# Attention rows turned to token order by 16-bit DMA transposes in place of TensorE transposes

## The chip, the cores and the metric

The kernel runs on one core of a Trainium2 chip. The metric is the device time of one execution in microseconds (us); lower is better. The core has a matrix engine (TensorE, PE in the profile; PEld is its weight load), a vector engine (VectorE, DVE), a scalar engine (ScalarE, ACT), a general engine (GpSimd, POOL) and a sync engine (SyncE, SP) that here only issues DMAs. Sixteen DMA engines serve all queues. The engines run their own instructions in program order and wait for each other by semaphores.

## What is computed

Attention with normalised queries and keys comes first, then a mixture of experts with a capacity. The batch is 8, with 12 heads, 448 positions and a head size of 64, so there are 3584 tokens of 768 values; 8 experts take at most 80 tokens each.

```python
q_n, k_n = (rmsnorm(q, g_q), rmsnorm(k, g_k))
scores = scale * np.matmul(q_n, k_n.transpose(0, 1, 3, 2))
attn = softmax(scores)
x = np.matmul(attn, v).transpose(0, 2, 1, 3).reshape(N, D)
...
logits = x @ w_gate
expert_idx = np.argmax(logits, axis=1)
gate_w = probs[np.arange(N), expert_idx]
for e in range(E):
    tok_idx = the tokens of expert e, the 80 of largest gate_w
    h = np.maximum(x[tok_idx] @ w1[e], 0.0)
    out[tok_idx] = gate_w[tok_idx, None] * (h @ w2[e])
```

All other rows of the output are zero.

## The kernel before

**Groups and half-steps.** The attention runs over 24 groups: a batch b and four of its heads, g = 3b + i. For each group, seven key blocks of 64 positions are gone through. The loop over `s` from -10 to NS + 5 (NS = 84) is a schedule written out by hand: in each half-step it scores two key blocks (`score`), adds up the exponentials of two earlier ones (`presum`) and multiplies two earlier ones with v (`av`). A group takes 3.5 half-steps. Everything else is hung into these half-steps with `at_slot`, in three places: `begins` (ahead of the scores; loads and other DMAs), `mid` and `end` (behind the products with v). b0 = 7g // 2 is a group's first half-step. Its q and k are loaded at b0 - 11, squared from b0 - 7, its v loaded at b0 - 4.

**The result of a group.** `av` gathers the unnormalised product in PSUM; at the group's last key block, in half-step b0 + 4, ACT copies it to the tile `us` of 128 partitions (two heads by 64 values) by 2 x 448 columns (positions), three buffers. Columns are positions and partitions are features there. The experts need rows: one token's 768 values together. `xout(g, u)` (L594 to L615) does that turn: PE transposes four blocks of 128 columns (L601) into the PSUM tile `xp`, of a pool of two buffers that it shares with the transposes of q and k (`tp`) and of the gate (`zt`); ACT copies `xp` to `xb` (L606), which has one buffer. It is called for u = 0 and u = 1 in two half-steps that follow each other. After the second, SP issues three DMAs (L614, L615) that store `xb` to the scratch `xr_scratch` in HBM; for the last group POOL issues them. A row of the scratch has 768 values and the 12 reciprocal sums of the token's softmaxes (`rz`, L418), as 32-bit floats.

**The gate.** From `us` and the sums, `zl` and the `gate` functions form logits, weights and, by ranking, the list of kept tokens of each expert. For batches 0 to 6 they lie among the half-steps of the next groups.

**The last batch and the experts.** Behind the loop stands a chain for the last batch, up to `idxG` (L835), the kept tokens. PE runs fillers meanwhile, `busy(n)`: n matmuls into the tile `hot` that nobody reads. Then POOL issues gathers by `idxG` from `xr_scratch` (L859), four ahead. `xpose(e)` multiplies the gathered rows by their reciprocal sums (`xn`, DVE, L868), transposes them on PE to `pxt` (L875) and copies them to `xgT` (DVE, L878). Each expert then runs a first product `ph` (L893) in two halves, each followed by ACT's `h_sb` (L897), then `xpose` of the next expert, then a second product `py` (L912); DVE scales it to `yo` (L917) and POOL scatters it to the output (L925).

**Weights and zeros.** The weights of experts 0 to 2 are loaded early. Those of experts 3 to 7 are cast to 16 bits in a scratch by POOL's DMAs during the attention (`stage_w`) and come in late from SP (`fetch_late`, L195); those of expert 5 in two parts, the first at L842 and L843, ahead of the gathers, behind a `memset` on DVE that holds it back. 28 DMAs of SP write zeros over the output.

Of the kernel before, what the change touches and what calls it, by code (L numbers as in the profile page):

```python
# [10 lines left out]
F32 = mybir.dt.float32  # L11
# [2 lines left out]
ALU = mybir.AluOpType  # L14
AX = mybir.AxisListType
U32 = mybir.dt.uint32
I32 = mybir.dt.int32
PSUM = bass.MemoryType.PSUM

# [2 lines left out]
def kernel(  # L22
# [36 lines left out]
    FC = F // 128  # L59


    XW = DM + H
    xr_dram = nc.dram_tensor("xr_scratch", (N, XW), F32, kind="Internal").ap()
    NW0 = 3
    wb_dram = nc.dram_tensor("wb_scratch", (E - NW0, 2, 128, DC * F), BF16,
                             kind="Internal").ap()
# [6 lines left out]
    ident = cpool.tile([128, 128], F32, name="ident")  # L73
# [97 lines left out]
    w_tiles = {}  # L171
# [30 lines left out]
    tpps = ctx.enter_context(tc.tile_pool(name="tp_ps", bufs=2, space=PSUM))  # L202
# [6 lines left out]
    prep = ctx.enter_context(tc.tile_pool(name="prep", bufs=2))  # L209
# [6 lines left out]
    with av_stack:  # L216
# [3 lines left out]
        st = [dict() for _ in range(NG)]  # L220
# [175 lines left out]
        def gate1v(b):  # L396
            zt = gst[b]["zt"]
            NT = NJ + 1
            ztv = zt[:, :].rearrange("p (j r) -> p j r", r=128)
            rz = gpool.tile([128, NT, H], F32, tag="rz", name="rz")  # L400
            for u in range(2):
                c = 64 * (1 - u)
                nc.vector.reciprocal(
                    rz[:].rearrange("p j (i u hh) -> p j u i hh", u=2, hh=2)[:, :, u],
                    ztv[:, :, c:c + 64].rearrange("p j (hh r) -> p j r hh", hh=2)[
                        :, :, 24:24 + NQ])
            lx = gpool.tile([128, NT, H, E], F32, tag="lx", name="lx", bufs=1)
            for u in range(2):
                for hh in range(2):
                    r = 64 * hh + 32 * u  # L410
                    nc.vector.tensor_mul(
                        lx[:].rearrange("p j (i k) e -> p j k i e", k=4)[:, :, 2 * u + hh],
                        ztv[:, :, r:r + NQ * E].rearrange("p j (i e) -> p j i e", e=E),
                        rz[:].rearrange("p j (i k) -> p j k i", k=4)[:, :, 2 * u + hh]
                        .unsqueeze(3).to_broadcast([128, NT, NQ, E]))
            gst[b]["lx"] = lx
            for t in range(2):
                (nc.sync if b < B - 1 else nc.gpsimd).dma_start(  # L418
                    out=xr_dram[b * S:(b + 1) * S, DM:XW].rearrange(
                        "(p x) h -> p x h", x=NX)[:, t::2],  # L420
                    in_=rz[64 * t:64 * t + 64, :NJ + 1 - t])

        def gate2(b):
            NT = NJ + 1
# [166 lines left out]
            return [[row, lambda: vbeat((0, 1))], [experts, lambda: vbeat((2, 3)), vtied],  # L591
                    [own, vahead], [counts, vput], [place], [turn]]

        def xout(g, u):  # L594

            b, i = divmod(g, NQ)
            xp = tpps.tile([128, 512], F32, tag="tp", name="xp")
            us = st[g]["us"]
            for j in range(NJ + 1):
                c = j * 128 if j < NJ else S - 128  # L600
                nc.tensor.transpose(xp[:, j * 128:(j + 1) * 128], us[:, u, c:c + 128],  # L601
                                    ident[:, :])
            if u == 0:
                st[g]["xb"] = prep.tile([128, NJ + 1, 256], F32, tag="xb", name="xb", bufs=1)
            xb = st[g]["xb"]
            nc.scalar.copy(xb[:, :, u * 128:(u + 1) * 128],  # L606
                           xp[:, :].rearrange("p (j d) -> p j d", d=128))
            if u == 0:
                return
            rows = xr_dram[b * S:(b + 1) * S, i * 256:(i + 1) * 256].rearrange(  # L610
                "(p x) d -> p x d", x=NX)
            eng = nc.sync if g < NG - 1 else nc.gpsimd
# [39 lines left out]
        for g in range(NG):  # L652
            b0 = g * RD // 2
            odd = g % 2
            at_slot(begins, max(b0 - 11, -10), load_qk, g)
            at_slot(begins, b0 - 4, load_v, g)
            if g:
                for a in range(2):
                    at_slot(mid, b0 - 7 + a if g > 1 else -1, square, g, a)
                    at_slot(end, b0 - 7 + a if g > 1 else -1, squares, g, a)  # L660
                at_slot(mid, b0 - 5 if g > 1 else 0, rstd, g)
                for a in range(2):
                    at_slot(mid, b0 - 5 + a if g > 1 else 0, normalise, g, a)
            for a in range(2):
                for f in range(2):
                    t = b0 - 4 + 2 * a + f
                    if g == 0 and a + f < 2 or g == 0 and a > f:
                        continue
                    if g < 2:
                        t += 2 if g == 1 and a + f == 0 else 1  # L670
                    at_slot(end, t, transp, g, a, f)
            at_slot(end, b0 + 4 + odd, xout, g, 0)
            at_slot(end, b0 + 5 + odd, xout, g, 1)
        for b in range(B):
            b0 = (NQ * b + NQ - 1) * RD // 2
            if b == B - 1:
# [67 lines left out]
    mpool = ctx.enter_context(tc.tile_pool(name="moe_sb", bufs=2))  # L744
# [12 lines left out]
    b = B - 1  # L757
# [26 lines left out]
    for j in range(NT):  # L784
        src = psb[:, 0, :] if j == 0 else row[:, :]
        c = min(j * 128 + 128, S)
# [41 lines left out]
    for k, (w, x) in enumerate(moves):  # L828
        for c0, c1, o in ((0, 3, 0), (3, 4, 1), (4, 5, 1)):
# [20 lines left out]
    xgs, xts = {}, {}  # L850
    def gather(e):

        if e % 4 == 3:
            xgs[e] = prep.tile([128, NJ + 1, 256], F32, tag="xb", name="xg", bufs=1)[
                :CAP].rearrange("p j d -> p (j d)")[:, :XW]
        else:
            xgs[e] = upool.tile([128, 2, S], F32, tag="us", name="xg")[:CAP].rearrange(
                "p u s -> p (u s)")[:, :XW]
        nc.gpsimd.indirect_dma_start(  # L859
            out=xgs[e], out_offset=None, in_=xr_dram[:, :],  # L860
            in_offset=bass.IndirectOffsetOnAxis(ap=idxG[:, e:e + 1], axis=0))

    def xpose(e):
        xg = xgs[e]
        xn = mpool.tile([CAP, DM], BF16, tag="xn", name="xn")
        for i in range(NQ):
            c = slice(256 * i, 256 * i + 256)
            nc.vector.tensor_mul(  # L868
                xn[:, c].rearrange("p (hh u d) -> p u hh d", hh=2, u=2),
                xg[:, c].rearrange("p (u hh d) -> p u hh d", hh=2, u=2),  # L870
                xg[:, DM + 4 * i:DM + 4 * i + 4].rearrange("p (u hh) -> p u hh", hh=2)
                .unsqueeze(3).to_broadcast([CAP, 2, 2, D]))
        pxt = mps.tile([128, DC, CAP], BF16, tag="pxt", name="pxt", bufs=1)
        for c in range(DC):
            nc.tensor.transpose(pxt[:, c, :], xn[:, c * 128:(c + 1) * 128],  # L875
                                identb[:CAP, :CAP])
        xgT = mpool.tile([128, DC, CAP], BF16, tag="xgT", name="xgT")
        nc.vector.tensor_copy(xgT[:], pxt[:])  # L878
        xts[e] = xgT

    for e in range(4):
        gather(e)
    xpose(0)
    busy(2)
    for e in range(E):
        w1_sb, w2_sb = w_tiles[e]
# [12 lines left out]
        if e + 1 < E:  # L899
            xpose(e + 1)  # L900
# [8 lines left out]
        for dn in range(2):  # L909
# [6 lines left out]
            c = DN if e + 1 < E or dn == 0 else DN // 2  # L916
# [5 lines left out]
        if NW0 + 3 + e < E:  # L922
# [42 lines left out]
```

## Time and profile before

Three executions took 476.2, 476.17 and 473.38 us; the median is 476.17.

| | us |
|---|---|
| median of three | 476.17 |
| profiled execution, time | 471.95 |
| its span in the profile | 469.9 |
| DVE copy xgT L878, mean of 8 (480 columns) | 0.41 |
| DVE reading py to yo L917, mean of 16 (384 columns) | 0.60 |
| ACT copy of 512 columns, L606 | 0.59 |
| ACT copy of 896 columns, us L346 | 0.90 |
| row stores of xb by SP, 192 KB and 64 KB, issue to landing | 7.0 and 5.3 |
| gathers xg, issue to landing, least and median | 3.4 and 8.2 |
| end of the last product with v, start of the tail | 402 |
| granted TensorE clock over the span | 0.989 |

A line of a group in the profile names the source line, the engine, the operation, the tile it writes and the tile it reads, sizes and count; behind the bar stand the busy time in us, the mean ns of one, and the engine's idle time ahead of it with what ended it. A line of the chain of waits is start, duration, engine, tile, line. A line of the timeline is start, duration and instruction, merged where equal ones follow each other; the brackets give the idle time before and its releaser. A line of stage sums has the busy us of PE, PEld, DVE, ACT and POOL, the granted clock, the share of the DMA engines' time and the GB/s.

### The profile page before, as it was taken

What the parts mean: (1) busy time and instruction counts of PE and PEld (TensorE: products, weight loads), DVE (VectorE), ACT (ScalarE), POOL (GpSimd) and SP (SyncE); (2) the same over time, 40 slices, a digit from 0 to 9 for tenths busy, and PEclk for the clock granted to TensorE, in tenths of its full rate; (3) what the DMA queues carried; (4) which work ended last, traced back from release to release, by engine and by line L of the source; (5) the groups of instructions that cost most, each with busy time, mean ns of one, the idle gap of its engine ahead of it and who ended that gap; (6) DMA issues with size and microseconds to landing.
All of it is one profiled execution on the core that took longest, in us unless ns stands there. A gap on an engine that the chain in (4) does not pass through costs nothing. (4 is left out here: it accounts for less than half of the span.)

```text
span 469.9 us, 11323 instructions
## 1 busy us (share of the span) xinstructions
PE 441.5 (94%) x4647; PEld 216.4 (46%) x4647; DVE 357.1 (76%) x650; ACT 326.6 (69%) x537; POOL 60.3 (13%) x123
## 2 busy tenths in 40 slices
PE   6999999999899999999899999898999999787995
PEld 6334444443344434443444444433444344345883
DVE  5798758996899778987898789868997767434561
ACT  6798877967688868886788688777888766301121
POOL 4010001200030004000400021001200010331421
PEclk9899999999999999999999999999999999979999
DMA  8999663996699766992899839956994377656991
GB/s 235 260 244 332 178 188 122 175 268 243 191 167 271 216 193 119 246 322 66 199 236 283 262 97 215 297 170 193 188 282 138 101 144 285 262 199 199 376 366 56
DMA packets 67530, 100.83 MB, mean 215 GB/s; under 512 B 7880, under 2 KB 59176, under 8 KB 66200
## 3 DMA queue, kind: packets, MB, share of 16 engines
q1 hardware_dynamic: 51184, 70.05, 46.2%
q0 software_dynamic: 16000, 29.61, 32.9%
q8 instruction: 36, 0.59, 0.5%
q10 hardware_dynamic: 296, 0.46, 0.3%
q14 instruction: 14, 0.11, 0.1%
HBM read 101.11 MB, written 39.89 MB: 300 GB/s over the span
## 5 line engine op out<-in xcount | busy, mean ns | idle before, releaser
L329 ACT ACTIVATE at<-ps 128x896 f32<-128x896 f32 x168 | 146.5, 922 | 14.4 <-PE ps L326 13.3
L326 PE MATMUL ps<-qkT 64*64 64x448 f32 x1344 | 149.2, 554 | 3.2 <-ACT zo L381 1.5
L341 PE MATMUL po<-at,vt 64*64 64x448 f32 x1344 | 144.4, 538 | 3.8 <-ACT us L346 3.8
L355 DVE TENSOR_TENSOR sm<-sm,at 128x896 f32<-128x896 f32 x120 | 130.6, 1089 | 3.3
L341 PEld LDWEIGHTS po<-at,vt 64*64 64x64 f32 x1344 | 49.8, 133 | 76.6 <-issue 66.0
L261 DVE TENSOR_REDUCE ms<-sq 128x14 f32<-128x896 f32 (+1 forms) x50 | 52.0, 1045 | 31.3 <-ACT sq L253 31.0
L326 PEld LDWEIGHTS ps<-qkT 64*64 64x64 f32 x1344 | 42.7, 132 | 66.9 <-issue 38.2
L289 DVE TENSOR_TENSOR qn<-qk,rs 128x896 f32<-128x896 f32 (+1 forms) x50 | 52.5, 1052 | 1.3
L301 PE MATMUL tp<-ident,qn 128*128 128x128 f32 x336 | 52.5, 280 | 0.0
L253 ACT ACTIVATE sq<-qk 128x896 f32<-128x896 f32 (+1 forms) x50 | 46.1, 925 | 2.8 <-DMA qk<-in_q_dram 2.1
L301 PEld LDWEIGHTS tp<-ident,qn 128*128 128x128 f32 x336 | 37.5, 142 | 14.6 <-ACT at L329 7.1
L606 ACT COPY xb<-xp 128x512 f32<-128x512 f32 x48 | 28.2, 587 | 20.5 <-PE xp L601 11.2
L471 POOL CAST pt<-gw 128x4 bf16<-128x4 f32 x8 | 1.5, 192 | 313.9 <-DVE gw L446 313.9
L897 ACT ACTIVATE h_sb<-ph 128x320 bf16<-128x320 f32 x16 | 7.0, 437 | 44.4 <-PE ph L893 44.4
L601 PEld LDWEIGHTS xp<-ident,us 128*128 128x128 f32 x192 | 20.5, 141 | 25.5 <-issue 18.4
L601 PE MATMUL xp<-ident,us 128*128 128x128 f32 x192 | 31.1, 284 | 0.5 <-ACT xb L606 0.5
L314 ACT ACTIVATE qkT<-tp,gqk 128x384 f32<-128x384 f32 (+1 forms) x47 | 30.1, 642 | 1.9 <-PE tp L301 1.9
L316 ACT COPY qkT<-tp 128x512 f32<-128x512 f32 (+1 forms) x48 | 25.7, 537 | 6.1 <-PE tp L301 5.7
L353 DVE TENSOR_TENSOR sm<-at 128x896 f32<-128x896 f32 x24 | 26.0, 1083 | 0.1
L346 ACT COPY us<-po 128x896 f32<-128x896 f32 x24 | 21.7, 904 | 6.1 <-PE po L341 6.0
L912 PE MATMUL py<-w_sb,h_sb 128*80 128x384 bf16 x128 | 22.2, 326 | 0.0
L372 PE MATMUL zl<-us,wgs 64*32 64x448 f32 x192 | 20.1, 541 | 1.0 <-ACT us L346 1.0
(168 smaller groups left out, 401.8 us busy)
## 6 DMA issues: line engine op xcount, KB each, us to landing
wb_scratch<-in_moe_w_dram POOLq DMA_DIRECT2D x20, 768.0 KB, 15.3
w_sb<-wb_scratch SPq DMA_DIRECT2D x10, 1536.0 KB, 13.9
vt<-in_v_dram SPq DMA_DIRECT2D x24, 448.0 KB, 7.2
out_dram<-zeros SPq DMA_DIRECT2D x28, 384.0 KB, 6.8
qk<-in_q_dram SPq DMA_DIRECT2D x23, 448.0 KB, 7.5
qk<-in_k_dram SPq DMA_DIRECT2D x23, 448.0 KB, 7.0
w_sb<-in_moe_w_dram POOLq DMA_DIRECT2D x6, 1536.0 KB, 20.0
xr_scratch<-xb SPq DMA_DIRECT2D x46, 192.0 KB, 7.0
```

Of the source, the lines that this page charges most:

```text
L253: nc.scalar.activation(st[g]["sq%d" % a][:, lo:hi], st[g]["qk"][a][:, lo:hi], AF.Square)
L261: nc.vector.reduce_sum(out=st[g]["ms"][:, a, lo:hi], in_=st[g]["sq%d" % a][:, lo:hi], axis=AX.X)
L289: nc.vector.tensor_mul(qn[:].rearrange("p (x hh) d -> p hh x d", hh=2)[:, h0:h1], qk[:, lo:hi].rearrange("p (hh x) d -> p hh x d", x=NX), ...
L301: nc.tensor.transpose(tp[:, x * 128:(x + 1) * 128], qn[:, 2 * (x0 + x):2 * (x0 + x) + 2].rearrange("p h d -> p (h d)"), ident[:, :])
L314: nc.scalar.activation(o, i, AF.Copy, scale=gqk[:, :])
L326: nc.tensor.matmul(ps[u * 64:u * 64 + 64, hh, :S], T1[d, u, x * 64:(x + 1) * 64], T0[d, u, :], start=True, stop=True)
L329: nc.scalar.activation(at[:], ps[:, :, :S], AF.Exp)
L341: nc.tensor.matmul(po[hh * D:(hh + 1) * D, u, :S], vt[p, hh * NX + x, :], at[p, hh, :], start=(x == 0), stop=(x == RD - 1))
L353: nc.vector.tensor_add(s["sm"][:], s["at0"][:], s["at1"][:])
L355: nc.vector.tensor_add(s["sm"][:], s["sm"][:], s["at%d" % x][:])
L601: nc.tensor.transpose(xp[:, j * 128:(j + 1) * 128], us[:, u, c:c + 128], ident[:, :])
L606: nc.scalar.copy(xb[:, :, u * 128:(u + 1) * 128], xp[:, :].rearrange("p (j d) -> p j d", d=128))
```

## The change

The scratch row becomes 1560 16-bit numbers of the same 3120 bytes: the low halves of the 768 values, their high halves, then the 12 reciprocal sums as before.

`xout` is replaced by two functions. `xturn(g)` lets SP issue two DMA transposes of `us`, seen as 128 partitions by 896 halves, for u = 0 and 1. In `xd` (one buffer, in the place of `xb`) each partition then holds one half, low or high by turns, of one token in each of the seven blocks. `xstore(g)` stores the even partitions and the odd ones by one DMA each, in runs of 256 halves (512 bytes) where there were 256 floats (1024 bytes). `xturn` stands at the end of half-step b0 + 4, `xstore` at the beginning of b0 + 6, for the last group at the end of b0 + 5 and on POOL.

Behind the gather, `xpose` joins the halves first: ACT copies the low ones and DVE the high ones into a new tile `xf` of 32-bit floats, every second 16-bit number each. The multiplications then read `xf`. In program order ACT's copy for the next expert stands behind both `h_sb` of the present one.

The first part of expert 5's weights, with its memset, moves from before the gathers to behind `xpose(0)`, and `busy(20)` at that place becomes `busy(12)`.

```diff
-    XW = DM + H
-    xr_dram = nc.dram_tensor("xr_scratch", (N, XW), F32, kind="Internal").ap()
+    XH = DM // NQ
+    XW = 2 * DM + 2 * H
+    xr_dram = nc.dram_tensor("xr_scratch", (N, XW), U16, kind="Internal").ap()
...
-        def xout(g, u):
...
-            for j in range(NJ + 1):
-                c = j * 128 if j < NJ else S - 128
-                nc.tensor.transpose(xp[:, j * 128:(j + 1) * 128], us[:, u, c:c + 128],
-                                    ident[:, :])
...
-            nc.scalar.copy(xb[:, :, u * 128:(u + 1) * 128],
-                           xp[:, :].rearrange("p (j d) -> p j d", d=128))
...
-            for t in range(2):
-                eng.dma_start(out=rows[:, t:SM // 64:2], in_=xb[64 * t:64 * t + 64, :NJ])
-            eng.dma_start(out=rows[:, NX - 1], in_=xb[64:, NJ])
+        def xturn(g):
+            us = st[g]["us"]
+            st[g]["xd"] = xd = prep.tile([128, NX, 2, 128], U16, tag="xb", name="xd", bufs=1)
+            for u in range(2):
+                nc.sync.dma_start_transpose(out=xd[:, :, u, :], in_=us[:, u, :].bitcast(U16))
+
+        def xstore(g):
             b, i = divmod(g, NQ)
+            xd = st[g]["xd"]
+            for h in range(2):
+                c = h * DM + i * XH
+                (nc.sync if g < NG - 1 else nc.gpsimd).dma_start(
+                    out=xr_dram[b * S:(b + 1) * S, c:c + XH].rearrange("(p x) d -> p x d", x=NX),
+                    in_=xd[h::2].rearrange("p x u d -> p x (u d)"))
...
-            at_slot(end, b0 + 4 + odd, xout, g, 0)
-            at_slot(end, b0 + 5 + odd, xout, g, 1)
+            at_slot(end, b0 + 4, xturn, g)
+            at_slot(begins if g < NG - 1 else end, b0 + (6 if g < NG - 1 else 5), xstore, g)
...
-    nc.vector.memset(w_tiles[NW0 + 2][0][:, 0, 0:2], 0.0)
-    fetch_late(NW0 + 2, (0, ))
-    busy(20)
+    busy(12)
...
     def xpose(e):
         xg = xgs[e]
+        xf = mpool.tile([CAP, DM], F32, tag="xf", name="xf")
+        halves = xf[:, :].bitcast(U16).rearrange("p (c h) -> p h c", h=2)
+        nc.scalar.copy(halves[:, 0], xg[:, :DM])
+        nc.vector.tensor_copy(halves[:, 1], xg[:, DM:2 * DM])
         xn = mpool.tile([CAP, DM], BF16, tag="xn", name="xn")
...
-                xg[:, c].rearrange("p (u hh d) -> p u hh d", hh=2, u=2),
+                xf[:, c].rearrange("p (u hh d) -> p u hh d", hh=2, u=2),
...
     xpose(0)
+
+    nc.vector.memset(w_tiles[NW0 + 2][0][:, 0, 0:2], 0.0)
+    fetch_late(NW0 + 2, (0, ))
     busy(2)
```

The store of `rz` and the gathered tiles only change their types and columns.

More of the change, by code (lines that the diff above doesn't have):

```diff
@@ L16 @@
 U32 = mybir.dt.uint32
+U16 = mybir.dt.uint16
 I32 = mybir.dt.int32
@@ L418, in gate1v @@
                 (nc.sync if b < B - 1 else nc.gpsimd).dma_start(
-                    out=xr_dram[b * S:(b + 1) * S, DM:XW].rearrange(
+                    out=xr_dram[b * S:(b + 1) * S, 2 * DM:XW].rearrange(
                         "(p x) h -> p x h", x=NX)[:, t::2],
-                    in_=rz[64 * t:64 * t + 64, :NJ + 1 - t])
+                    in_=rz[64 * t:64 * t + 64, :NJ + 1 - t].bitcast(U16))
         def gate2(b):
@@ L592, in merge @@
                     [own, vahead], [counts, vput], [place], [turn]]
-        def xout(g, u):
-            b, i = divmod(g, NQ)
-            xp = tpps.tile([128, 512], F32, tag="tp", name="xp")
-            us = st[g]["us"]
-            for j in range(NJ + 1):
-                c = j * 128 if j < NJ else S - 128
-                nc.tensor.transpose(xp[:, j * 128:(j + 1) * 128], us[:, u, c:c + 128],
-                                    ident[:, :])
[L603 to L606, printed above, removed]
-                           xp[:, :].rearrange("p (j d) -> p j d", d=128))
[L608 to L612, printed above, removed]
-            for t in range(2):
-                eng.dma_start(out=rows[:, t:SM // 64:2], in_=xb[64 * t:64 * t + 64, :NJ])
-            eng.dma_start(out=rows[:, NX - 1], in_=xb[64:, NJ])
+        def xturn(g):
[4 more added lines that the diff above has]
+        def xstore(g):
+            b, i = divmod(g, NQ)
+            xd = st[g]["xd"]
[4 more added lines that the diff above has]
+                    in_=xd[h::2].rearrange("p x u d -> p x (u d)"))
         def weights_early():
@@ L853, in gather @@
         if e % 4 == 3:
-            xgs[e] = prep.tile([128, NJ + 1, 256], F32, tag="xb", name="xg", bufs=1)[
-                :CAP].rearrange("p j d -> p (j d)")[:, :XW]
+            xgs[e] = prep.tile([128, NX, 2, 128], U16, tag="xb", name="xg", bufs=1)[
+                :CAP].rearrange("p x u d -> p (x u d)")[:, :XW]
         else:
             xgs[e] = upool.tile([128, 2, S], F32, tag="us", name="xg")[:CAP].rearrange(
-                "p u s -> p (u s)")[:, :XW]
+                "p u s -> p (u s)").bitcast(U16)[:, :XW]
         nc.gpsimd.indirect_dma_start(
@@ L869, in xpose @@
                 xn[:, c].rearrange("p (hh u d) -> p u hh d", hh=2, u=2),
-                xg[:, c].rearrange("p (u hh d) -> p u hh d", hh=2, u=2),
-                xg[:, DM + 4 * i:DM + 4 * i + 4].rearrange("p (u hh) -> p u hh", hh=2)
+                xf[:, c].rearrange("p (u hh d) -> p u hh d", hh=2, u=2),
+                xg[:, 2 * DM:].bitcast(F32)[:, 4 * i:4 * i + 4].rearrange("p (u hh) -> p u hh", hh=2)
                 .unsqueeze(3).to_broadcast([CAP, 2, 2, D]))
```

## The prediction

> **What bounds the kernel now.** I first read the busy totals, then the sums over the attention stage (16 to 402 us), then the groups the change removes, and last the tail as a chain and a timeline.
>
> ```profile
> PE 441.5 (94%) x4647; PEld 216.4 (46%) x4647; DVE 357.1 (76%) x650; ACT 326.6 (69%) x537; POOL 60.3 (13%) x123
> ```
> ```profile
> 16.00:402.00 386.00, 375.47 (x3917) 169.16 (x3913) 318.19 (x538) 304.92 (x496) 34.66 (x72) 1.00 0.81 207
> ```
> ```profile
> L606 ACT COPY xb<-xp 128x512 f32<-128x512 f32 x48 | 28.2, 587 | 20.5 <-PE xp L601 11.2
> L601 PE MATMUL xp<-ident,us 128*128 128x128 f32 x192 | 31.1, 284 | 0.5 <-ACT xb L606 0.5
> ```
> ```profile
> 375.80 1.50 PE po L341 x16
> 377.30 0.59 PE xp L601 x4
> 377.89 0.44 PE tp L301 x4
> ```
> In attention PE is busy for 375 of 386 us, DVE for 318, ACT for 305, and the DMA engines for 81% (the figure before the GB/s). PE bounds this stage, and every four transposes of xp hold its chain for 0.59 us. DVE and DMA are the next nearest to full.
>
> The tail is a different stage. It waits for the first gather and then runs on PE:
> ```profile
> 417.32 8.36 DMA xg<-xr_scratch,idxG
> ```
> ```profile
> 432.14 1.88 PE L893 MATMUL ph<-xgT,w_sb 128*128 128x80 bf16 x48
> 432.87 1.08 DVE L868 TENSOR_TENSOR xn<-xg 80x256 bf16<-80x256 f32 x3
> 433.20 0.44 ACT L897 ACTIVATE h_sb<-ph 128x320 bf16<-128x320 f32 x1 [3.24 <-PE ph L893]
> 433.85 0.40 PE L875 MATMUL pxt<-identb,xn 80*128 80x80 bf16 x6
> 434.06 0.44 ACT L897 ACTIVATE h_sb<-ph 128x320 bf16<-128x320 f32 x1 [0.42 <-PE ph L893]
> 434.09 1.31 PE L912 MATMUL py<-w_sb,h_sb 128*80 128x384 bf16 x7
> ```
> This is expert 1, as start, duration and instruction. PE's program order is ph of this expert, pxt of the next, py of this one. DVE makes the next expert's xn during ph, so pxt never holds PE up. The pause from ph's end (434.02) to py is 0.07 us, and the next expert starts 4.55 us after this one (436.69).
>
> [...]
>
> **The change, part by part.** The sum is made against the profiled execution, 471.95 us with a span of 469.9. That is 4.2 us under the median of 476.17, so I take the difference and apply it to the median.
>
> *1. PE transposes and ACT copies go.* 48 quadruples at 0.59 us in the chain are 28.3 us at most. From one start to the next such a group costs 0.49 (377.23 to 377.72 on PE's timeline), so 48 make 23.5 us. ACT loses 48 x 587 ns = 28.2 us, but it isn't the bound. DVE's 318 us in a stage of 362 would be 88%, so a little comes back as waits on DVE: I take **-22**, between 18 and 28.
>
> *2. DMA transposes come in, hidden or not.* SP issues 48 of them, each 128 x 896 x 2 B = 229 KB. They start when us is copied, one or two half-steps before the old stores. Each group's pair must land before its two stores go out. The stores must land before the next pair may write, because xd has one buffer. So each group has a loop of pair plus stores, and its period is now 386/24 = 16.1 us, 15.2 once part 1 is taken off. Stores: today 7.0 us for 192 KB and 5.3 for 64 KB. They become two of 224 KB with twice the packets, half the size; I take 7.5 and allow 9 (28 more packets per engine at the mean 68 ns of the hardware queue, 46.2% x 469.9 x 16 / 51184, are 1.9 us). Pair: [...] with some 3 us of landing (what the 9 to 12 KB stores of rz take), [...] I take 5[...]. The loop is then 12.5 of 15.2 us: **0**, covered by PE's work, if barely. Behind SP's new waits stand the loads of v, q and k and the zeros of the output. A q or k load goes out 11 half-steps ahead of its scores and four ahead of its squares, v four ahead of its scores. A half-step is 16.1/3.5 = 4.6 us, so four are 18 us against 7 to 7.5 of landing. That is slack of some 11 us. SP already waits for the xb copies before these same loads (141 us of its waits name that line).
>
> *3. The tail's join.* Each expert gets an ACT copy and a DVE copy of 80 x 768 halves. None such is in the trace. ACT takes 587 ns for 512 columns and 922 for 896, so by line about 810; DVE about the same (408 for 480 16-bit columns), beside it. [...] For expert 0 it lies in the open: **+0.9** with the handover. For experts 1 to 7 its place decides: ACT's program order has the copy for expert e+1 behind both h_sb of expert e, and the second waits for the last ph. So after ph ends: h_sb 0.48, copy 0.81, xn 1.08 with 0.07 of handover, the last pxt about 0.2, then py. That is 2.6 us in place of 0.07, with pxt inside it and PE idle, as py stands behind pxt. 7 x 2.5 = **+17.7**; with copies of 0.4 and 1.3 us it is 15 to 21.
>
> *4. The weights of expert 5 step behind the gathers.* The first 1.5 MB of them was issued at 417.07, just ahead of the gather, which then took 8.36 us; the fastest gather of this run lands in 3.4. I take 4.2: **-4.2**. The last group's stores may land up to 1 us later than today's 416.12 (pair issued from 403.1 in the place of PE's transposes, landed by 408, then POOL's 1.3 for the stores and 1.3 for rz, whose DMAs land in 6.5): **+0.5**. Later weights cost nothing: expert 5 comes five periods of 7.1 us later. The memset of their tile moves behind expert 0's xgT on DVE, which has room. busy(12) at the cold 0.43 us ends near 421.7, so the array stays about as idle ahead of the first pxt as now: 0.
>
> Sum: -22 + 0 + 0.9 + 17.7 - 4.2 + 0.5 = **-7.1**, so 464.9 against 471.95, and 476.17 - 7.1 = **469**. With the bounds of parts 1, 3 and 4 this case spans 460 to 478.
>
> **The rivals.** *A, the loop of xd becomes the bound (slower).* One mechanism: pair plus stores exceed the period of 15.2 us, in the attention loop, on SP. Each us above costs 23 us, one for each following group; it turns the sum to a loss from a loop of 15.5. With stores of 7.5 that is a pair of 8 us. At 9 us: 16.5, so 469 + 1.3 x 23 = 499. [...]
> *B, the DMA engines fill up (slower).* In 386 us they are busy 0.81, 313 us. [...] the extra 10,752 packets up to 46 at 68 ns over 16 engines; I take 15. [...] the sum is +7: 483. Against it: [...]0.98 in 20 to 60 us stopped nothing (PE 39.1 of 40).
> *C, ACT's place costs nothing.* If the copy were ready in time the tail would pay only 0.9: 469 - 17.7 = 451. Against it stands the program order on ACT and PE.
> That the change doesn't do what it says is excluded as far as the instruction order shows: no xp is left on PE, and 48 transposes stand on SP.
>
> **How the numbers follow.** Forecast 0.52, A 0.23, B 0.15, C 0.10. About 1% (4.8 us, so 471.4 and 480.9) is what a measurement of this kernel can tell from no change. Of the forecast's 0.52, 0.37 lies below 471.4, 0.13 within and 0.02 above: faster 0.37 + 0.10 = 0.47, same 0.13, slower 0.02 + 0.23 + 0.15 = 0.40. The range 453 to 500 leaves out most of C and the far half of A.
>
> **What would show it.** Right: xp and xb gone, attention ended near 380 us, ps following tp directly; SP's wait ahead of the row stores ended by transposes in about 5 us; in the tail a wait of PE's pxt weight load on DVE xn of some 2.5 us per expert, which DVE in turn spends on ACT's xf, and a period near 7.1 us; the first gather landing in about 4 us. Wrong: SP waiting for row stores before each transpose and PE waiting for q, k or v (A); DMA at 1.0 throughout with landings well above 7 us (B); an expert period still near 4.6 (C); or a PE clock of 0.50 in the tail, which would add about 2 us for each half-speed ph.

## The result and the profile after

The changed kernel takes 509.15 us (median of four, 506.88 to 510.9) against 475.6 us before (473.38 to 476.2). The ratio is 1.071, with a 95% interval of 1.065 to 1.078. It is slower, and outside the range. Two executions much longer than the others of their kernels, 1026.12 and 478.83 us, are left out of the medians and ratios of the experiments below.

The profiled executions took 471.95 and 510.81 us, 3.7 under and 1.7 over these medians, so their spans differ by some 5 us more than the medians do. They are split against each other here. "us(23)" is the start of ACT's last copy of us.

| stretch | before | after | difference | predicted |
|---|---|---|---|---|
| to us(23) | 402.1 | 414.5 | +12.4 | -22 |
| us(23) to the first gather's issue | 15.2 | 22.7 | +7.5 | +0.5 |
| first gather, issue to landing | 8.36 | 3.60 | -4.8 | -4.2 |
| landing to the first ph | 1.9 | 3.2 | +1.3 | +0.9 |
| first ph to the end | 42.3 | 65.1 | +22.8 | +17.7 |
| span | 469.9 | 509.1 | +39.2 | -7.1 |

Of the 46.3 us between the sum of the forecast and this one, the attention stage has 34.4. First the busy totals of the page and the sums over the stage (length, then PE, PEld, DVE, ACT, POOL busy, clock, DMA share, GB/s), for the changed kernel:

```profile
PE 437.0 (86%) x4447; PEld 201.6 (40%) x4447; DVE 362.0 (71%) x658; ACT 311.7 (61%) x497; POOL 60.0 (12%) x122
```
```profile
16.00:416.00 400.00, 365.89 (x3752) 152.12 (x3752) 318.40 (x538) 285.32 (x451) 34.66 (x72) 0.97 1.01 225
```

PE has less to do (365.9 us in place of 375.5), yet the stage is longer: its pauses grew from 10.5 to 34.1 us. The DMA share is 1.01 where it was 0.81, at only 225 GB/s. What PE's pauses go back to is seen in the groups of the page, as idle time of ACT ahead of the squares of q and k, before and after:

```profile
L253 ACT ACTIVATE sq<-qk 128x896 f32<-128x896 f32 (+1 forms) x50 | 46.1, 925 | 2.8 <-DMA qk<-in_q_dram 2.1
```
```profile
L256 ACT ACTIVATE sq<-qk 128x896 f32<-128x896 f32 (+1 forms) x50 | 46.0, 923 | 27.5 <-DMA qk<-in_q_dram 27.2
```

At the longest of these waits the timeline shows PE waiting for ACT in turn. listT stands behind sq in ACT's order:

```profile
269.20 0.95 ACT L256 ACTIVATE sq<-qk 128x896 f32<-128x896 f32 x1 [11.29 <-DMA qk<-in_q_dram]
270.05 0.20 ACT L593 COPY listT<-mp 24x80 bf16<-24x80 bf16 x1
```
```profile
270.30 1.77 PE L329 MATMUL ps<-qkT 64*64 64x448 f32 x8 [9.54 <-ACT listT L593]
```

The loads of q come late. They are issued by SP, and SP's waits (line waited for, us in total, times, longest) say where it stands meanwhile:

```profile
SPq L610 <- DMA xd<-us: 91.5, 25, 13.9
...
SPq L603 <- DMA xr_scratch<-xd: 45.2, 15, 10.8
```

L610 is the row store. For 91.5 us SP stands at the head of its queue until the pair of transposes has landed in xd. Standing is not a loss by itself: the kernel before stood longer at this place, 141.3 us, but for ACT, so it was ahead of the work, and its loads of q still came in time (2.1 us of ACT's waits).

```profile
SPq L614 <- ACT qkT L316: 141.3, 16, 12.6
```

The timeline of SP in the changed kernel shows one ordinary pair, one long one, and what is behind the long one; POOL's line shows what ran beside it:

```profile
167.71 4.74 SPq L603 DMA_TRANSPOSE xd<-us  x2
175.65 1.20 SPq L610 DMA_DIRECT2D xr_scratch<-xd  x2
176.94 0.59 SPq L228 DMA_DIRECT2D vt<-in_v_dram  x1
...
181.28 5.14 SPq L603 DMA_TRANSPOSE xd<-us  x2
197.98 1.69 SPq L610 DMA_DIRECT2D xr_scratch<-xd  x2
199.72 0.64 SPq L704 DMA_DIRECT2D out_dram<-zeros  x1
200.45 2.10 SPq L228 DMA_DIRECT2D vt<-in_v_dram  x1
```
```profile
184.64 3.04 POOL L192 DMA_DIRECT2D wb_scratch<-in_moe_w_dram  x4
```

From the start of a pair to its stores it is 7.9 us in the first case and 16.7 in the second, where POOL pushes four staging DMAs of 768 KB at once (it had waited 51.15 us for `gw` of the gate). The next load of v leaves 23.5 us after the one before, where a group has 15 to 16. The change's transposes are cut into packets of 256 bytes. The 1792 packets of an ordinary pair are over within 2.2 to 4.3 us; those of this pair took 12.6 us, in which 1155 staging packets ran too, of 134 or 172 ns each (medians of the two sizes). Three more pairs met such a burst, and the longest held SP for 27.0 us, from 233.8 to its stores at 260.8.

### The profile page after: what moved, and what is told of

The parts are those of the page before. It is cut to its first block, busy times and chain, and to the rows that moved or that the text cites. A ratio compares the mean times of both kernels' runs of the same rounds, so it can differ in the third digit from the quotient of the medians.

```text
span 509.1 us, 10888 instructions
## 1 busy us (share of the span) xinstructions
PE 437.0 (86%) x4447; PEld 201.6 (40%) x4447; DVE 362.0 (71%) x658; ACT 311.7 (61%) x497; POOL 60.0 (12%) x122
## 4 chain that ended last, share of the span: by engine, by line
PE 47%; DMA 18%; DVE 17%; issue 9%; ACT 6%; POOL 1%; SPq 1%; POOLq 0%; DVEq 0%; ACTq 0%
PE po L344 16%; PE ps L329 16%; DMA qk<-in_q_dram 6%; PE tp L304 5%; DMA xd<-us 5%; DMA qk<-in_k_dram 4%; DVE sm L358 4%; PE zl L375 4%; DVE qn L292 3%; DVE ms L264 2%; PE py L913 2%; DMA xr_scratch<-rz 2%; PE ph L894 2%; ACT us L349 1%; ACT at L332 1%
## 5 line engine op out<-in xcount | busy, mean ns | idle before, releaser
L329 PE MATMUL ps<-qkT 64*64 64x448 f32 x1344 | 155.7, 572 | 21.1 <-ACT listT L593 18.4
L332 ACT ACTIVATE at<-ps 128x896 f32<-128x896 f32 x168 | 146.3, 919 | 22.7 <-PE ps L329 20.9
L344 PE MATMUL po<-at,vt 64*64 64x448 f32 x1344 | 147.0, 547 | 7.2 <-ACT us L349 7.2
L256 ACT ACTIVATE sq<-qk 128x896 f32<-128x896 f32 (+1 forms) x50 | 46.0, 923 | 27.5 <-DMA qk<-in_q_dram 27.2
L304 PE MATMUL tp<-ident,qn 128*128 128x128 f32 x336 | 55.6, 290 | 0.0
L304 PEld LDWEIGHTS tp<-ident,qn 128*128 128x128 f32 x336 | 36.4, 143 | 39.8 <-issue 23.6
L913 PE MATMUL py<-w_sb,h_sb 128*80 128x384 bf16 x128 | 25.3, 357 | 0.0
L349 ACT COPY us<-po 128x896 f32<-128x896 f32 x24 | 21.6, 898 | 5.2 <-PE po L344 5.2
L873 PE MATMUL pxt<-identb,xn 80*128 80x80 bf16 x48 | 6.1, 214 | 20.8 <-DVE xn L866 19.6
L918 DVE TENSOR_SCALAR yo<-py,gwT 80x384 f32<-80x384 f32 (+1 forms) x16 | 9.6, 601 | 17.4 <-PE py L913 17.4
L866 DVE TENSOR_TENSOR xn<-xf,xg 80x256 bf16<-80x256 f32 x24 | 8.7, 417 | 16.9 <-ACT xf L861 16.9
## 6 DMA issues: line engine op xcount, KB each, us to landing
w_sb<-wb_scratch SPq DMA_DIRECT2D x10, 1536.0 KB, 12.4
```

Of the source, the lines that this page charges most:

```text
L256: nc.scalar.activation(st[g]["sq%d" % a][:, lo:hi], st[g]["qk"][a][:, lo:hi], AF.Square)
L304: nc.tensor.transpose(tp[:, x * 128:(x + 1) * 128], qn[:, 2 * (x0 + x):2 * (x0 + x) + 2].rearrange("p h d -> p (h d)"), ident[:, :])
L329: nc.tensor.matmul(ps[u * 64:u * 64 + 64, hh, :S], T1[d, u, x * 64:(x + 1) * 64], T0[d, u, :], start=True, stop=True)
L332: nc.scalar.activation(at[:], ps[:, :, :S], AF.Exp)
L344: nc.tensor.matmul(po[hh * D:(hh + 1) * D, u, :S], vt[p, hh * NX + x, :], at[p, hh, :], start=(x == 0), stop=(x == RD - 1))
L349: nc.scalar.copy(st[g]["us"][:], po[:, :, :S])
```

## The experiments

Single profiles of attention scatter. Four profiles have the attention code of the change (itself, its repeat, and two kernels that differ only behind the loop or in its last half-steps); their us(23) are 414.5, 413.6, 417.8 and 407.1. Differences below some 10 us between single profiles of this stage are therefore not read as effects. Times of single runs carry the tail's scatter too (last experiment of the tail), and the median of the kernel before lay between 475.6 and 478.9 us beside these runs (483.1 in one single run), so attention is judged by us(23).

### Attention: what the transposes cost, and by what way

**Transposes left out**

```diff
-                nc.sync.dma_start_transpose(out=xd[:, :, u, :], in_=us[:, u, :].bitcast(U16))
...
-            xd = st[g]["xd"]
+            xd = st[g]["us"][:].rearrange("p u s -> p (u s)").bitcast(U16).rearrange(
+                "p (x d) -> p x d", x=NX)
```

> The DMA transposes are left out and the two stores of each group take their bytes straight from us, so the stored rows are not turned; packets, loads, staging and order stay. The join reads the halves in pairs. If the transposes cost the attention its time (by packets between those of the staging, or by filling the DMA engines), the last us copy ends at 380 to 388 us, where before had it at 403 and the change at 415, and the whole is 471 to 480. If the smaller store packets or the stores' new place do it, it ends at 405 or later and the whole stays above 495.

us(23), from the lines of the copy, of the kernel before (L346), of this one and of the changed one (L349; min, median and max in ns, then first and last start):

```profile
L346 ACT COPY us<-po x24: 887/906/909, 30.0 to 402.1; 128x896 f32<-128x896 f32 x24
```
```profile
L349 ACT COPY us<-po x24: 887/906/907, 31.2 to 386.3; 128x896 f32<-128x896 f32 x24
```
```profile
L349 ACT COPY us<-po x24: 877/906/908, 30.5 to 414.5; 128x896 f32<-128x896 f32 x24
```

So taking the PE transposes away brings 15.8 us, and putting the DMA transposes in costs 28.2. us(23) came as expected for a cost of the transposes; the time, 485.61, did not (471 to 480).

The 28.2 us are not spread over the groups. Copy by copy, the changed kernel's us falls behind this one's by 5.7 us at group 8 (counted from 0) and by 12.6 at groups 14 and 15, and by at most 2.1 at any other group; its repeat has 7.0 and 12.6 at the same groups. The pairs of groups 6 and 12, two groups ahead, are the two that the bursts of staging stretched most (17.3 and 22.3 us from first packet to last). The other two stretched pairs, of groups 9 and 18 (12.6 and 16.3 us), are followed by 2.1 and 1.7 us.

**Staging DMAs put behind a pair**, each held on POOL by a small copy that reads xd:

```diff
+        def stage_behind(g, e, i, half):
+            nc.gpsimd.tensor_copy(tick[:, :], st[g]["xd"][:, NX - 1, 1, 0:4])
+            stage_w(e, i, half)
...
-                    at_slot(begins, 2 + 5 * (2 * e + i) + 2 * half, stage_w, e, i, half)
+                    g = 2 + 4 * (e - NW0) + 2 * i + half
+                    at_slot(end, g * RD // 2 + 4, stage_behind, g, e, i, half)
```

> Each of the 20 staging DMAs of the late weights waits on POOL for one pair of transposes (a small POOL copy that reads xd), so a burst of staging can no longer run beside a pair; the bytes moved are the same. Theory of the interleaving ([...] a pair takes 12 to 22 us): no pair takes over 6 us, the last us copy ends at 385 to 393 us, the whole is 480 to 488. Rival, the DMA engines are simply full: pairs go on being slow somewhere or loads get late, the last us copy ends at 408 or later, the whole is above 502.

us(23) went to 424.5 and the time to 536.36; the expected 385 to 393 was missed. Every pair is now short (packets over within 2.1 to 4.8 us), and SP's wait at the stores fell to 52.6 us. But the staging now leaves at the same moment as the row stores, which share SP's loop and for which the next pair waits, and as the loads behind them: a load of q lands in 9.6 us (median) in place of 6.0, and ACT's wait for q grew to 44.0 us.

```profile
SPq L603 <- DMA xr_scratch<-xd: 78.3, 17, 9.4
...
SPq L616 <- DMA xd<-us: 52.6, 23, 4.4
```

With the bursts away from the pairs, none takes over 4.8 us where four took 12.6 to 22.3; but moving them to this place only moves the collision.

**Plain DMAs of the same shape**, which do not turn anything:

```diff
-                nc.sync.dma_start_transpose(out=xd[:, :, u, :], in_=us[:, u, :].bitcast(U16))
+                nc.sync.dma_start(out=xd[:, :, u, :], in_=us[:, u, :].bitcast(U16).rearrange(
+                    "p (x d) -> p x d", x=NX))
```

> Each DMA transpose becomes a plain DMA of the same bytes between the same tiles, in the same 256-byte pieces, with the same waits; the rows are not turned and the join reads the halves in pairs. If the 256-byte pieces and the order of the queue cost the time, the last us copy ends where the change had it, 410 to 420 us, and pairs that meet the staging take over 12 us again. [...] the pairs are shorter and the last us copy ends at 395 or earlier.

us(23) 403.4, between the two expectations (410 to 420, and 395 or earlier for a price of the transposing itself), time 510.55. Against the kernel without transposes 17.1 of the 28.2 us are there without any transposing. SP's wait at the stores is even 118.9 us, as SP issues a plain DMA in 0.67 us where it needs 2.07 for a transpose (medians). The other 11 us are hardly more than the scatter, and two pairs met a burst here where four did in the changed kernel, so in us(23) a price of the transposing itself is not shown. In the packets it is: the same 43,008 packets of 256 bytes took 51.6 us of all 16 engines' time here and 84.0 as transposes. A plain DMA that SP waits for at this place costs most of the loss.

**No zeros over the output** (28 DMAs of 384 KB fewer on SP's queue):

```diff
-        for i in range(N // 128):
+        for i in range(0):
```

> The 28 DMAs that write zeros over the output are left out: 35 us of all sixteen DMA engines' time, the transposes and their order unchanged. Theory of the full DMA engines: the attention gets shorter by 15 us or more, the last us copy ends at 400 or earlier. Theory of the order (the queue of SP stands while a pair or its stores land, whatever the load): it stays within 6 us of 415.

us(23) 391.0, time 499.54. With less load 23.5 of the 28.2 us come back. Load matters, but this run doesn't tell it from the order, because a lighter load also shortens the waits in SP's queue (64.6 us at the stores in place of 91.5), and none of its pairs met a burst (4.8 us at most).

**Stores a half-step and a half later, still one buffer**

```diff
-            at_slot(begins if g < NG - 1 else end, b0 + (6 if g < NG - 1 else 5), xstore, g)
+            at_slot(mid if g < NG - 1 else end, b0 + (7 if g < NG - 1 else 5), xstore, g)
```

> The row stores are moved one half-step later, behind the loads of v, q and k of that half-step in SP's order; one buffer xd as in the change. If loads are late because they stand behind the wait for a pair, ACT's waits for q (27 us in the change) fall below 10 us and the last us copy ends at 405 or earlier. If the loop of the one buffer (pair, stores, next pair) sets the period, it ends at 412 or later, since the stores come later in it.

us(23) 420.7, time 530.37. The wait at the stores is gone (16.3 us), but the pair of the next group now stands behind stores that have only just left:

```profile
SPq L603 <- DMA xr_scratch<-xd: 143.0, 26, 10.5
```

With one buffer, as this run has it, the stores can't be late enough for the pair and early enough for the next pair.

**Two buffers for xd, stores where the change has them.** The attention pool gives up one of seven buffers for the room.

```diff
-    apool = av_stack.enter_context(tc.tile_pool(name="attn", bufs=7))
+    apool = av_stack.enter_context(tc.tile_pool(name="attn", bufs=6))
...
-            st[g]["xd"] = xd = prep.tile([128, NX, 2, 128], U16, tag="xb", name="xd", bufs=1)
+            st[g]["xd"] = xd = prep.tile([128, NX, 2, 128], U16, tag="xb", name="xd", bufs=2)
```

> The change with two buffers for xd alone, stores at b0 + 6 as in the change. If what makes the loads of q, k and v late is the loop of the one buffer (a pair waits for the stores before it), the last copy of us starts at 393 to 400 in place of 414.5. If it is the stores' wait for their own pair, at the head of SP's queue, a second buffer takes nothing of it away: 408 or more.

> Two buffers for xd alone, again. If the first 406.5 was no more than scatter, the last copy of us starts at 404 to 418 here; if the second buffer alone brings some 8 us, at 404 to 408 again.

us(23) 406.5 and, repeated, 410.6: not clear of the scatter of one buffer. SP waits at the stores for 83.8 us in the first of the two. The loop of the one buffer alone is not the cause.

**Two buffers and later stores**, in the middle of b0 + 9 and then of b0 + 7:

```diff
-            at_slot(begins if g < NG - 1 else end, b0 + (6 if g < NG - 1 else 5), xstore, g)
+            at_slot(mid if g < NG - 1 else end, b0 + (9 if g < NG - 2 else 7 if g < NG - 1 else 5), xstore, g)
```

> Two buffers xd, and a group's stores go behind the next group's pair in SP's order, so that a pair has a whole period to land and no pair waits for the last stores; the attention tiles go from seven buffers to six to make room. If order and the single buffer are the cause, the last us copy ends at 385 to 395. If the DMA engines are full, it stays at 408 or later with a DMA share near 1.0.

> Two buffers for xd and the stores at the middle of b0 + 7, a half-step and a half later than in the change. If the place of the stores in SP's order decides (SP stands at them until their own pair has landed, with the loads of v, q and k behind), the last copy of us starts between the 394 of the stores at b0 + 9 and the 406 of those at b0 + 6, about 399. If b0 + 9 helps only since it avoids the bursts of POOL's staging, 404 or more.

us(23) 393.8 with b0 + 9 and 390.0 with b0 + 7 (times 501.62 and 494.86). The second is 3.7 us from the kernel that has no transposes at all. SP's waits of it:

```profile
SPq L228 <- DVE qn L292: 58.6, 20, 6.4
...
SPq L610 <- DMA xd<-us: 15.2, 9, 5.6
```

The wait at the stores fell from 91.5 to 15.2 us, and SP's largest wait is now one for buffers that qn gives free: the loads have become early, and ACT's wait for q fell from 27.2 to 3.8 us. SP's time for issuing the transposes is not the cause: it is 152.9 us in all here and 120.4 in the changed kernel. The repaired versions below, with the stores of nearly all groups at b0 + 9 too, have 394.5 and 395.8. The sums over 30 to 390 us, of the changed kernel and of this one:

```profile
30.00:390.00 360.00, 327.24 (x3339) 136.21 (x3335) 288.21 (x486) 258.62 (x411) 30.59 (x64) 0.97 1.01 224
```
```profile
30.00:390.00 360.00, 345.53 (x3620) 146.01 (x3619) 306.08 (x519) 272.24 (x432) 34.06 (x71) 0.99 1.09 238
```

The whole kernels move the same bytes; in this stretch the second moves more, at a higher DMA share (1.09), and PE pauses for 14.5 us in place of 32.8. So a share of 1.01 was not the most that the DMA engines give; with the same bytes, another order reached 1.09.

What the order does has two parts that these runs don't separate. With b0 + 7, SP stands less at the stores; and its pairs of groups 6, 9 and 12, issued earlier, miss the bursts that they met in the changed kernel. The two pairs that still meet one, of groups 15 and 18 (17.6 and 15.2 us), are followed by losses of 2.4 and 1.6 us. At the first of them the loads of v, q and k leave from 282.3 us on, behind the pair's issuing, and no longer wait for its stores, which leave at 294.5.

That the way goes by the loads of q is seen over all 15 profiles that have the change's stores. Their us(23) runs from 386.3 to 424.5. Less ACT's wait for q it lies between 380.5 and 393.4.

### The tail

**The join one expert ahead**, so that ACT has the halves copied before the present expert's h_sb ask for it:

```diff
-    def xpose(e):
+    def join(e):
...
+    def xpose(e):
+        xg, xf = xgs[e], xfs[e]
...
+        if e + 2 < E:
+            join(e + 2)
```

> The ACT and DVE copies that join the halves are moved one expert ahead in program order, so that ACT's copy no longer stands between h_sb and xn of the next expert; nothing else moves. Theory of the place: the period of an expert falls from 7.15 to about 4.6 us, 7 x 2.5 = 17.5 us less: 490 to 493. Rival, the join itself is too much work for ACT or DVE or the clock stays low: the period stays above 6 us, the whole above 500.

The time was 498.26 although us(23) came at 417.8. Behind the first expert the period is 5.7 us three times and then 5.0 (starts of ph at 447.39, 453.61, 459.29, 464.99, 470.64, 475.61, 480.60, 485.58), in place of 7.15. So the place on ACT cost 1.5 to 2.2 us per expert. The expected 4.6 was missed; what is left above 4.55 appears in the next experiment too.

**The move of expert 5's weights alone**, in the kernel before:

```diff
-    nc.vector.memset(w_tiles[NW0 + 2][0][:, 0, 0:2], 0.0)
-    fetch_late(NW0 + 2, (0, ))
-    busy(20)
+    busy(12)
...
+    nc.vector.memset(w_tiles[NW0 + 2][0][:, 0, 0:2], 0.0)
+    fetch_late(NW0 + 2, (0, ))
```

> The kernel before with one part of the change alone: the first part of expert 5's weights goes behind the first expert's turn, and 12 fillers in place of 20. If it keeps its gain when alone, the first gather lands in about 4 us in place of 8.4 and the whole is 3 to 4 us shorter, 472 by the median. Rival: the weights come too late or the clock is cold in the first expert, and it is level or slower.

473.26 us (median of three) against 478.37, ratio 0.987 (0.981 to 0.994). The first gather lands in 3.54 us in place of 8.36. Part comes back: the period of the experts is 5.7 and 5.0 us here too, where it was 4.55, with no join in the kernel. The second h_sb of an expert starts up to 1.3 us later behind its ph, and DVE's xgT up to 1.9 us behind the recorded end of pxt, where it was 0.04. What delays them is not shown.

**The last group's stores on SP, straight behind their pair, and the late weights behind them**

```diff
-                (nc.sync if g < NG - 1 else nc.gpsimd).dma_start(
+                nc.sync.dma_start(
...
-        at_slot(end, NS - 3, weights_early)
+        at_slot(begins, NS - 1, weights_early)
```

> The change with the last group's stores on SP behind their pair in place of POOL, and the late weights issued after them, one buffer as in the change. If POOL's wait for the last pair and the landing beside the weights cost the 5.5 us and 2 us between the tokens' list and the first gather, the gather is issued within 2 us of the list, and the span is 5 to 8 us below that of the change, 501 to 504. If the list itself is late for another reason, the span stays at 507 or more.

The gather is issued 15.7 us after us(23), in place of 22.7: the 7 us of the change were a late last pair, POOL's wait for it and a slow landing, as the chain of waits of the changed kernel has it (start, duration, what):

```profile
421.70 2.99 DMA xd<-us
...
425.28 0.45 POOL xr_scratch L610
425.73 0.23 issue
425.96 0.79 POOL xr_scratch L610
426.75 0.48 POOL xr_scratch L421
427.23 8.74 DMA xr_scratch<-rz
...
437.18 3.60 DMA xg<-xr_scratch,idxG
```

The last pair itself leaves only at 420.3, as SP waits 10.8 us for the stores of the group before, which land beside the weights of expert 3. POOL stands at the store (L610) until the pair has landed, and its stores of rz (L421) come next in its order; that of 12 KB lands in 9.2 us, beside the weights of expert 4, where the one of the kernel before took 6.6. But in this experiment the span rose to 511.5, and the expected 501 to 504 were missed: the weights now run beside the gather (8.53 us), and the experts take 7.7 to 10.6 us each, much as in the next run.

**The change again, unaltered**

> The change again, unaltered, for the scatter of one profile: in three kernels with its attention code the last copy of us began at 414.5, 407.1 and 417.8. I expect 407 to 418 and a time of 506 to 511.

us(23) 413.6, but a time of 521.53. PE's timeline of one expert, in the first profile and in this repeat:

```profile
461.29 1.88 PE L894 MATMUL ph<-xgT,w_sb 128*128 128x80 bf16 x48
465.08 0.92 PE L873 MATMUL pxt<-identb,xn 80*128 80x80 bf16 x6 [1.91 <-DVE xn L866]
465.84 2.77 PE L913 MATMUL py<-w_sb,h_sb 128*80 128x384 bf16 x16
```
```profile
463.69 1.88 PE L894 MATMUL ph<-xgT,w_sb 128*128 128x80 bf16 x48
468.80 0.92 PE L873 MATMUL pxt<-identb,xn 80*128 80x80 bf16 x6 [3.23 <-DVE xn L866]
469.55 4.45 PE L913 MATMUL py<-w_sb,h_sb 128*80 128x384 bf16 x16
```

The instructions are the same. In the first the pause ahead of pxt is 1.91 us and py takes 2.77; in the repeat the pause is 3.23 and py takes 4.45, with a granted clock of 0.57 from 471.0 to 473.8. The next expert starts 7.15 us later in the one and 10.14 in the other: 1.3 of the pause and 1.7 of py are the difference. A slow py follows shorter pauses too, and not each time: pauses of 1.91 us in the first profile are followed by a py of 2.77 us five times and of 4.45 and 4.22 once each, with a granted clock of 0.50 from 450.3 to 453.6 and from 474.2 to 477.5; pauses of 2.49 in the repeat by 2.77 twice and 4.45 once. In the kernel before, whose clock was 0.50 from 415.0 to 421.7, a pause of 2.60 us ahead of the first pxt (426.19) left it at 1.00. So the length of the pause alone doesn't decide, and what does is not shown. The experts of the kernel before leave PE idle for 0.07 us at this place, and its granted clock is 1.00 from 421.8 to 469.5. With the join's wait, low clocks stand among the experts (the 0.50 of the first profile, the 0.57 of the repeat), at different experts in each. The 1.3 us of longer pause have the size of the late h_sb of the experiment with part 4 alone, and are as open.

### Versions with all parts repaired

Two buffers, stores at b0 + 9, the last stores on SP, the join one expert ahead and the late weights later; in the second version expert 4's weights also go behind expert 0's transposes:

```diff
+    for i in range(2):
+        nc.vector.memset(w_tiles[NW0 + 1][i][:, 0, 0:2], 0.0)
+    fetch_late(NW0 + 1)
```

> The change with two buffers for xd, the stores held back to b0 + 9, the last stores issued by SP straight behind their pair, the join of an expert one expert ahead and the weights of expert 4's late part moved away from the last stores. If the loss of the change was the order and the one buffer in attention, plus the join's place, plus the last stores, then each part comes back as in its own run: last copy of us near 393, first gather issued near 409, expert period 4.6 to 5.0, span near 457 and a time of 459 to 465, faster than the kernel before. Rival: the DMA engines are full (a share above 1.0), so what leaves one place comes back in another: then the time is 475 or more.

> The best version so far, with expert 4's weights also issued only behind expert 0's transposes. If the gather of 8.69 us there is long because these 3 MB run beside it, it lands in 3.4 to 4.5 us, the experts start some 4 us earlier and the span is near 464, the time near 465 (ratio to before about 0.97). Rival: the weights are then late (12.6 MB at the 380 GB/s of that stage are 33 us, from about 414 to 448), PE waits for w_sb, and the time is 469 or more.

The first takes 469.18 us (median of three) against 476.79, ratio 0.981 (0.974 to 0.987): 1.3 to 2.6% faster than the kernel before, and so faster than both. The 459 to 465 that were summed up were missed; its gather takes 8.69 us beside the weights. The second takes 471.67 against 478.91, ratio 0.984 (0.977 to 0.992), no better. Its gather lands in 3.42 us and the first ph starts at 418.69 (422.47 in the first version), but the last ph starts later, 459.08 against 458.35. PE waits for weights there:

```profile
450.56 1.89 PE L904 MATMUL ph<-xgT,w_sb 128*128 128x80 bf16 x48 [0.49 <-DMA w_sb<-wb_scratch]
459.08 1.89 PE L904 MATMUL ph<-xgT,w_sb 128*128 128x80 bf16 x48 [1.51 <-DMA w_sb<-wb_scratch]
```

In the last experts of this version PE waits for the transfer of the late weights; the rival expected of this run held. The intervals of both versions overlap with that of the kernel before with part 4 alone (0.987), so it isn't shown that turning x by DMA is worth anything by itself.

## Why the prediction was wrong

**Part 1 (-22): right in kind, too large.** Without any transposes the stage is 15.8 us shorter. PE's busy time fell by 21 us (375.5 to 354.4), but its pauses rose from 10.5 to 17.6. The prediction took 1.5 us off for waits; it was 7.

**Part 2 (0): the step that failed.** It cost 28.2 us. The loop's sum was near, in part by luck. The 5 us for a pair were the author's estimate; the trace of the kernel before has no DMA transpose. An ordinary pair with SP's issuing takes 7.9 us (a transpose lands in 5.6, the median of its issues), and stores land in 3.9, not 7.5, so the loop is 11.8 us of 15.2 outside the bursts, where 12.5 was written. What was wrong is the sentence that covered the loads behind it. "That is slack of some 11 us" was compared with a pair of 5 us alone. In fact SP, which issues in order, takes about 5 us to issue the two transposes and stood 91.5 us at the stores, up to 13.9 at once. Beside a staging burst, which stands in no term of the sum, a pair held it for 16.7 to 27.0 us, more than the slack, and most of the loss falls two or three groups behind such pairs. ACT's wait for q grew from 2.1 to 27.2 us. The prediction saw that loads stand behind the wait and then priced it at zero. SP's 141 us before were no proof that this is harmless: those waits were for ACT's qkT, by an SP that was ahead of the work.

**Rival A** gave 499, near the result, by a mechanism that is only half right. The second buffer, which removes its loop, brought nothing clear of the scatter by itself, and so did later stores without it; the two together brought 21 to 25 us. The place of the wait in SP's queue, beside the bursts, is where the cause lies, and the one buffer is what forbids the better place.

**Rival B** (engines fill up) saw the share of 1.01 correctly, and is refuted as the bound: 1.09 ran with 18 us fewer pauses. Its sum of +7 rested on the author's estimate of what the transposes ask of the engines; they took 84.0 us of all 16 engines' time. Load is part of the mechanism, as the bursts (pairs of 12.6 to 22.3 us) and the run without zeros (23.5 us back) show, and not a limit reached.

**Part 3 (+0.9 and +17.7): the mechanism was right.** The period became 7.15 us, where 4.55 + 2.5 was written. From the groups of the page:

```profile
L873 PE MATMUL pxt<-identb,xn 80*128 80x80 bf16 x48 | 6.1, 214 | 20.8 <-DVE xn L866 19.6
...
L866 DVE TENSOR_TENSOR xn<-xf,xg 80x256 bf16<-80x256 f32 x24 | 8.7, 417 | 16.9 <-ACT xf L861 16.9
```

PE waits for DVE's xn and DVE for ACT's xf, as named. ACT's copy took 1.03 us in place of 0.81. Of the 22.8 us, 18.2 are seven periods of +2.6; the other 4.6 are mostly two slow experts (starts 10.15 and 8.56 us apart) with the clock at 0.73 to 0.76 over the 7 us stretches around them, which the text had only as a warning. **Rival C** is refuted.

**Part 4 (-4.2): right for the gather** (-4.8). The +0.5 for the last stores is wrong by 7 us: it counted POOL's issuing, but neither that the last pair waits for the stores before it, nor that rz's stores and the token list stand behind POOL's wait for the last pair, nor that rz's stores land beside the weights of expert 4 (8.74 us in the chain). "Later weights cost nothing" isn't borne out either: with this part alone the experts' period grew from 4.55 us to 5.0 and 5.7, for a cause that is open.

## What to carry to other kernels

When a DMA result is consumed by another DMA of the same queue, ask what stands behind the second one: here SP stood for 91.5 us in all until the first had landed, and ACT's wait for the loads of q behind it grew from 2.1 to 27.2. Put the second one far enough behind that the data is there (here, with two buffers, b0 + 7 in place of b0 + 6 left 15.2 us of a wait of 83.8), and count the buffers this takes; here buffer and place brought 21 to 25 us together and nothing clear apart. A wait that is short on average is to be priced at its worst case, beside the largest burst of another queue, against the slack of what is queued behind it. In a stage of short pauses, look at the granted clock behind each new wait: here two of seven pauses of 1.91 us were followed by a py of 4.2 to 4.5 us in place of 2.77, at a clock of 0.50.

## What was not expected of the hardware

Halving the packets of the row stores cost little: 20,608 packets of 512 bytes took 39.0 us of all 16 engines' time where 10,304 of 1024 bytes took 37.0.

The transposes' 43,008 packets of 256 bytes took 84.0 us, a mean of 31.2 ns at a median of 18. As plain DMAs the same packets took 51.6 us, a mean of 19.2 at the same median. The difference lies in few packets: 1059 of the transposes' took more than 40 ns, up to 3.1 us and 31.8 us of the 16 engines in all; of the plain ones 100 did, 0.5 us in all. What holds them up is not shown.

The packets of a pair, 459 KB, took 2.17 us at the least, some 211 GB/s, and 1.84 us (some 250) in the kernel with two buffers and stores at b0 + 7. At the mean under load it is 131 GB/s (24 pairs of 459 KB in 84.0 us), where the plain DMAs of the same shape have 213.
